# Block 8 of the attention stage: sigmoid issued ahead of block 0's layer norm, val chains in the four accumulator banks, conv in two halves

## The chip, the cores and the metric

One NeuronCore of a Trainium2 chip. Its engines are TensorE (PE in the profile, with its weight loads as PEld), VectorE (DVE), ScalarE (ACT), GpSimd (POOL) and SyncE (SP, which only issues DMAs here). The metric is the device time of one execution in microseconds; lower is better.

## The reference, cut to what matters

Three parts run one after the other over 4608 rows (8 x 576) of 512 channels: chunked attention, a gated convolution layer, and a layer norm with a feed-forward layer. The change lies at the seam of the second and third.

```python
x = attention(q, k, v)                              # chunks of 64, 8 heads of 64
gate = sigmoid(sum(conv_w[k] * x shifted by 4-k))   # 5 taps along the rows, per channel
y = (gate * (x @ w_val)) @ w_out
xn = (y - mean) / sqrt(var + 1e-6) * g_ln
out = y + relu(xn @ w_ch1) @ w_ch2
```

## The kernel before, in words

The rows are cut into 9 blocks of 512 (`BLK`, index j, 0 to 8), and each block into two units of 256 (`UN`, index u, 0 to 17). A loop over slots issues the first two parts: slot u computes unit u's scores (`a3`), transposes unit u-1's probabilities (`a4`) and multiplies them with v (`a5`, L208), which leaves the attention output of the block in `xf`, `xh` and `xl` with channels on partitions: four tiles of 128 channels, index f. The dense work of a block is spread over later slots by `at(slot, part, work)` (L655 to L672): `conv` (L243), `sigm` (L255), `val` (L266) and `proj` (L286).

- `conv(j, f, half)`: one ACT instruction (L248) and four DVE instructions (L250) over 512 columns, in place in `cg`. `half` 2 is all columns, 0 and 1 are the halves. Block 0 uses halves; all others are whole. There is one buffer of `cg`, shared by all blocks.
- `sigm(j)`: one ACT instruction over all of `cg` (L257).
- `val(j, f)`: a chain of 12 matmuls (three products per input tile, since each operand is split in a high and a low part) into one PSUM bank. Then DVE multiplies it with the gate (`gv`, L279), ACT copies the high part (`gh`, L282) and DVE subtracts to get the low part (`gl`, L283).
- `proj(j, t)`: a chain of 12 matmuls into one PSUM bank for 128 rows; ACT copies it to `y` (L296, two buffers) and issues the store to `y_dram` (L297).

All these chains take their bank from `ps_d`, a pool of two banks that are used in turn. PSUM has eight; the other six belong to `a3`, `a4` and `a5` until `prep()` (L620), called at the end of slot 18, closes their pools and opens `ps_t` (two banks, for transposes) and `acc` (four banks `acc0` to `acc3`, for the second feed-forward matmul, `ff2` at L372).

`prep()` also starts the third part for block 0: it loads block 0's `y` into `yt0` (L633), normalises four tiles of 128 rows (`ln_rows`, L317: statistics on DVE, a square root on ACT at L328, small DVE operations, then ACT at L337), transposes them on PE (`turn_rows`, L345), copies them out on ACT (L347), splits them into high and low (`high_low`, L389 and L390) and loads `yt0` again (L637). The first feed-forward matmul `ff1` (L354, tile `psh`) of block 0 reads the result.

What sets the order: from slot 4 on to the end of the slots, a planner orders each engine's queue. It runs through a model of the machine and takes, of what is ready, the work with the smallest place in program order; `tc.high_priority()` moves a piece's place forward. Each queue then runs strictly in that order on the chip. In the feed-forward part PE's order is the program's.

After the slots, `s_d.close()` (L684) gives back the memory of the weights `vh`, `vl`, `oh`, `ol` and of block buffers. The pools of the feed-forward part lie in the same memory and wait for its last readers tile by tile. There the weights of the feed-forward part are decoded, 16 tile pairs in all: loaded (L122, L127), decoded by ACT (L87) and three DVE passes (L88 to L90), split by ACT (L95) and POOL (L96). Those of the first four pairs are ready early; most of the rest run from 360 to 433 us.

Of the kernel before, what the change touches and what calls it, by code (L numbers as in the profile page):

```python
# [8 lines left out]
F32 = mybir.dt.float32  # L9
# [10 lines left out]
def tile_chunk_attention_gated_mlp(ctx: ExitStack, tc: tile.TileContext, qk, v, w_val, conv_w, w_out, g_ln, w1, w2, out):  # L20
# [10 lines left out]
    P = 128  # L31
    BLK = 512
    UN = 256
    UPB = BLK // UN
    NB = NT // BLK
# [12 lines left out]
    def boundary(j):  # L48
        o = (-(j * BLK)) % S
        return o if 0 < o < BLK else BLK  # L50
# [5 lines left out]
    ps_d = ctx.enter_context(tc.tile_pool(name="ps_d", bufs=2, space=PSUM))  # L56
# [186 lines left out]
    def conv(j, f, half):  # L243
        n = BLK + (HALO if boundary(j) < BLK else 0)
        x = xf[j]
        lo, hi = ((0, BLK // 2), (BLK // 2, n), (0, n))[half]
        o = cg[:, f, lo:hi]
        nc.scalar.activation(out=o, in_=x[:, f, lo:hi], func=ACTF.Copy, scale=cw[:, f:f + 1])  # L248
        for i in range(1, KC):
            nc.vector.scalar_tensor_tensor(  # L250
                out=o, in0=x[:, f, i + lo:i + hi], scalar=cw[:, i * CT + f:i * CT + f + 1], in1=o,
                op0=ALU.mult, op1=ALU.add,
            )

    def sigm(j):  # L255
        n = BLK + (HALO if boundary(j) < BLK else 0)
        nc.scalar.activation(out=cg[:, :, :n], in_=cg[:, :, :n], func=ACTF.Sigmoid)  # L257
# [3 lines left out]
    def chain(ps, ops):  # L261
        n = len(ops)
        for i, (lt, rh) in enumerate(ops):
            nc.tensor.matmul(out=ps, lhsT=lt, rhs=rh, start=(i == 0), stop=(i == n - 1))  # L264

    def val(j, f):  # L266
        hs, ls = wv["vs"]
        fs = slice(f * P, (f + 1) * P)
        ps = ps_d.tile([P, BLK], F32, tag="d", name="psv")
        ops = []  # L270
        for c in range(CT):
            ops += [(hs[c][:, fs], xh[j][:, c, :]), (hs[c][:, fs], xl[j][:, c, :]), (ls[c][:, fs], xh[j][:, c, :])]
        chain(ps, ops)
        o = boundary(j)
        gv = pD2.tile([P, BLK], F32, tag="gv", name="gv")
        with tc.high_priority():
            for lo, hi, sh in ((0, o, 0), (o, BLK, HALO)):
                if lo < hi:
                    nc.vector.tensor_tensor(out=gv[:, lo:hi], in0=ps[:, lo:hi], in1=cg[:, f, lo + sh:hi + sh], op=ALU.mult)  # L279
            a = pD1.tile([P, BLK], F32R, tag=f"gh{f}", name="gh")  # L280
            b = pD1.tile([P, BLK], F32R, tag=f"gl{f}", name="gl")
            nc.scalar.activation(out=a, in_=gv, func=ACTF.Copy)  # L282
            nc.vector.tensor_tensor(out=b, in0=gv, in1=a, op=ALU.subtract)  # L283
        gh[j, f], gl[j, f] = a, b

    def proj(j, t):  # L286
        hs, ls = wv["os"]
        ts = slice(t * P, (t + 1) * P)
        ps = ps_d.tile([P, DM], F32, tag="d", name="pso")
        ops = []  # L290
        for f in range(CT):
            ops += [(gh[j, f][:, ts], hs[f]), (gh[j, f][:, ts], ls[f]), (gl[j, f][:, ts], hs[f])]
        chain(ps, ops)
        y = pD2.tile([P, DM], F32, tag="y", name="y")
        with tc.high_priority():
            nc.scalar.activation(out=y, in_=ps, func=ACTF.Copy)  # L296
            nc.scalar.dma_start(out=y_dram[j][ts, :], in_=y)  # L297
# [4 lines left out]
    p2 = {}  # L302
# [14 lines left out]
    def ln_rows(ys):  # L317

        n = len(ys)
        mv = p2["b"].tile([P, n, 2], F32, tag="mv", name="mv")  # L320
        for t, y in enumerate(ys):
            s6 = p2["b"].tile([P, nc.vector.BN_STATS_DIM], F32, tag="s6", name="s6")
            nc.vector.bn_stats(out=s6, in_=y)
            nc.vector.bn_aggr(out=mv[:, t, :], in_=s6)
        ve = p2["b"].tile([P, n], F32, tag="ve", name="ve")
        nc.vector.tensor_scalar(out=ve, in0=mv[:, :, 1], scalar1=1e-6, scalar2=None, op0=ALU.add)
        r = p2["b"].tile([P, n], F32, tag="r", name="r")
        nc.scalar.activation(out=r, in_=ve, func=ACTF.Sqrt)  # L328
        nc.vector.reciprocal(out=r, in_=r)
        w = p2["b"].tile([P, n], F32, tag="w", name="w")  # L330
        nc.vector.tensor_tensor(out=w, in0=r, in1=r, op=ALU.mult)
        nc.vector.tensor_tensor(out=w, in0=w, in1=ve, op=ALU.mult)
        nc.vector.tensor_scalar(out=w, in0=w, scalar1=-0.5, scalar2=1.5, op0=ALU.mult, op1=ALU.add)
        nc.vector.tensor_tensor(out=r, in0=r, in1=w, op=ALU.mult)
        nc.vector.scalar_tensor_tensor(out=w, in0=mv[:, :, 0], scalar=-1.0, in1=r, op0=ALU.mult, op1=ALU.mult)
        for t, y in enumerate(ys):
            nc.scalar.activation(out=y, in_=y, func=ACTF.Identity, scale=r[:, t:t + 1], bias=w[:, t:t + 1])  # L337
        return ys

    def turn_rows(ys, i):  # L340

        for t, y in enumerate(ys):
            ps = ps_t.tile([P, CT, P], F32, tag="t", name="pst")
            for c in range(CT):
                nc.tensor.transpose(out=ps[:, c, :], in_=y[:, c * P:(c + 1) * P], identity=ident)  # L345
            for c in range(CT):
                nc.scalar.activation(  # L347
                    out=p2["xt"][:, c, (i + t) * P:(i + t + 1) * P], in_=ps[:, c, :], func=ACTF.Copy,
                    scale=cw[:, KC * CT + c:KC * CT + c + 1],
                )  # L350
# [19 lines left out]
    acc = {}  # L370
# [17 lines left out]
    def high_low(hi, lo, a, eng):  # L388
        nc.scalar.activation(out=hi, in_=a, func=ACTF.Copy)  # L389
        eng.tensor_tensor(out=lo, in0=a, in1=hi, op=ALU.subtract)  # L390
# [223 lines left out]
    def at(u, i, fn):  # L614
        dense.setdefault((u, i), []).append(fn)
# [4 lines left out]
    def prep():  # L620
        nonlocal xn0, yt0, ps_t
        s_a.close()
        ps_t = ctx.enter_context(tc.tile_pool(name="ps_t", bufs=2, space=PSUM, reuse_waits="tile"))
        p2["b"] = ctx.enter_context(tc.tile_pool(name="p2c", bufs=2, side="right", reuse_waits="tile"))
        pX = ctx.enter_context(tc.tile_pool(name="p2x", bufs=1, side="right", reuse_waits="tile"))
        p2["xt"] = pX.tile([P, CT, 2 * BLK], F32, name="xt")
        p2["0"] = s_0.enter_context(tc.tile_pool(name="p2a", bufs=1, side="right", reuse_waits="tile"))
        p2["h"] = s_0.enter_context(tc.tile_pool(name="p2h", bufs=2, side="right", reuse_waits="tile"))
        p2["acc"] = ctx.enter_context(tc.tile_pool(name="acc", bufs=1, space=PSUM, reuse_waits="tile"))
        xn0 = [p2["0"].tile([P, CT, BLK], F32R, name=f"xn{i}") for i in range(2)]  # L630
        yt0 = p2["0"].tile([P, HB, DM], F32, name="yt0")
        y0 = y_dram[0].rearrange("(t p) d -> p t d", p=P)
        nc.sync.dma_start(out=yt0, in_=y0)  # L633
        with tc.high_priority():
            ln_rows([yt0[:, i, :] for i in range(HB)])
        turn_rows([yt0[:, i, :] for i in range(HB)], 0)
        nc.sync.dma_start(out=yt0, in_=y0)  # L637
        for i in range(0, HB, 2):
            ts = slice(i * P, (i + 2) * P)
            high_low(xn0[0][:, :, ts], xn0[1][:, :, ts], p2["xt"][:, :, ts], nc.vector)  # L640
# [17 lines left out]
    for j in range(NB):  # L658
        u = UPB * (j + 1) + LAG - 1
        for f in range(CT):  # L660
            if j == NB - 1:
                at(u, 3, lambda j=j, f=f: conv(j, f, 2))
            elif j:
                at(*[(u, 3), (u, 3), (u + 1, 1), (u + 1, 1)][f], lambda j=j, f=f: conv(j, f, 2))
            else:
                at(u - 1, 3, lambda j=j, f=f: conv(j, f, 0))
                at(*[(u, 3), (u, 3), (u + 1, 0), (u + 1, 0)][f], lambda j=j, f=f: conv(j, f, 1))
        at(u + 1, 2, lambda j=j: sigm(j))
        for f in range(CT):
            at(*[(u + 1, 2), (u + 1, 3), (u + 2, 0), (u + 2, 1)][f], lambda j=j, f=f: val(j, f))  # L670
        for t in range(BLK // P):
            at(*[(u + 2, 2), (u + 2, 3), (u + 3, 0), (u + 3, 1)][t], lambda j=j, t=t: proj(j, t))  # L672
# [5 lines left out]
    for u in range(NU + LAG + 4):  # L678
        if u == MANUAL:
            head.close()  # L680
        slot(u)
        if u == NU + LAG - 1:
            prep()
    s_d.close()  # L684
    p2["w"] = ctx.enter_context(tc.tile_pool(name="wB", bufs=1, reuse_waits="tile"))
# [108 lines left out]
```

## Time and profile before

| | us |
|---|---|
| median of three runs | 1152.28 |
| lowest and highest of the three | 1148.00, 1153.68 |
| the profiled execution | 1149.92 |
| its span, first to last instruction | 1148.1 |
| PE busy in the span | 1076.7 (94%) |
| DVE busy | 710.6 (62%) |
| ACT busy | 483.1 (42%) |

The profiled execution's own time is 1.8 us more than its span. Busy time of an engine adds up instructions; a matmul of 512 columns is shown with 0.39 us though the next starts 0.23 us later at full clock, so PE's rate is read from the starts. PEclk is the clock granted to PE as a share of 2.4 GHz.

### The profile page before, as it was taken

How to read it: one execution, taken by the hardware profiler on the slowest of the kernel's cores; microseconds unless marked ns; L12 is line 12 of the kernel's file. 1: busy time of each engine (PE TensorE's matmuls, PEld its weight loads, DVE VectorE, ACT ScalarE, POOL GpSimd, SP SyncE). 2: the span in 40 equal slices, each digit the busy share in tenths (PEclk: the TensorE clock that was granted, in tenths of full speed). 3: DMA queues.
4: the chain of work that ended last, by engine and by line, in shares of the span. 5: the costliest groups of instructions: out<-in, count | busy, mean ns of one | idle time of the engine just before them, and what ended most of it. 6: DMA issues, size and time to landing. Idle time of an engine off the chain costs nothing.

```text
span 1148.1 us, 17073 instructions
## 1 busy us (share of the span) xinstructions
PE 1076.7 (94%) x6862; PEld 876.1 (76%) x6862; DVE 710.6 (62%) x1155; ACT 483.1 (42%) x828; POOL 110.8 (10%) x120
## 2 busy tenths in 40 slices
PE   5788989899869899899999999999999999999998
PEld 5676768777758787688887888887888888878877
DVE  6999899888664978555556544356444347432434
ACT  3566666556563665434534224333223324121221
POOL 2021010000002443322320000000000000000000
PEclk9799999999879999999999999999999999999999
DMA  8445546531123672723442723332623222722211
GB/s 330 167 127 168 176 140 211 172 132 56 41 89 133 209 235 80 250 110 127 148 148 92 238 91 124 97 110 92 227 85 129 101 74 97 233 92 83 83 37 74
DMA packets 58581, 155.28 MB, mean 135 GB/s; under 512 B 5742, under 2 KB 13958, under 8 KB 56198
## 3 DMA queue, kind: packets, MB, share of 16 engines
q1 hardware_dynamic: 53318, 144.75, 37.3%
q10 hardware_dynamic: 5184, 9.44, 2.2%
q8 instruction: 54, 0.88, 0.3%
q14 instruction: 25, 0.20, 0.1%
HBM read 116.41 MB, written 37.75 MB: 134 GB/s over the span
## 4 chain that ended last, share of the span: by engine, by line
PE 64%; DVE 23%; ACT 5%; issue 4%; DMA 3%; POOL 0%; SPq 0%; ACTq 0%; POOLq 0%; DVEq 0%
PE acc L496 15%; PE x L522 15%; PE psf L496 14%; PE zy L522 10%; DVE cg L250 7%; PE psv L264 5%; DVE da L90 2%; DVE da L89 2%; DVE sm L176 1%; PE acc L382 1%; DVE xl L238 1%; DVE h L534 1%; PE psh L264 1%; DVE pr L179 1%; DVE gv L279 1%
## 5 line engine op out<-in xcount | busy, mean ns | idle before, releaser
L542 DVE TENSOR_TENSOR c<-x,c 128x512 f32<-128x512 f32 x96 | 66.2, 690 | 236.9 <-ACT c L538 180.6
L496 PE MATMUL acc<-w,h 128*128 128x512 f32 x768 | 186.1, 391 | 0.0
L496 PE MATMUL psf<-w,h 128*128 128x512 f32 x768 | 186.0, 391 | 0.0
L496 PEld LDWEIGHTS acc<-w,h 128*128 128x128 f32 x768 | 144.2, 188 | 31.4
L496 PEld LDWEIGHTS psf<-w,h 128*128 128x128 f32 x768 | 144.2, 188 | 31.3
L522 PE MATMUL x<-t,wc 128*128 128x512 f32 x576 | 148.1, 393 | 3.4 <-DVE c L542 3.4
L538 ACT ACTIVATE c<-zy 128x512 f32<-128x512 f32 x96 | 57.9, 603 | 187.4 <-PE zy L522 187.2
L522 PEld LDWEIGHTS x<-t,wc 128*128 128x128 f32 x576 | 108.8, 189 | 27.8 <-DVE c L542 4.6
L533 ACT ACTIVATE h<-c 128x512 fp32r<-128x512 f32 x96 | 60.5, 631 | 136.3 <-DVE c L542 135.8
L250 DVE SCALAR_TENSOR_TENSOR cg<-xf,cw,cg 128x516 f32<-128x516 f32 (+2 forms) x160 | 106.3, 706 | 0.0
L501 DVE TENSOR_TENSOR yt<-psf,yt 128x512 f32<-128x512 f32 x128 | 88.2, 691 | 25.1 <-PE psf L496 21.1
L522 PE MATMUL zy<-b,wc 128*128 128x512 f32 x384 | 98.9, 393 | 0.0
L264 PE MATMUL psv<-xh,vh 128*128 128x512 f32 x144 | 64.2, 446 | 22.6 <-DVE gv L279 22.6
L522 PEld LDWEIGHTS zy<-b,wc 128*128 128x128 f32 x384 | 71.2, 188 | 14.6
L534 DVE SCALAR_TENSOR_TENSOR h<-c,h 128x512 fp32r<-128x512 f32 x96 | 68.4, 713 | 14.1 <-ACT h L533 13.9
L96 POOL TENSOR_TENSOR w<-da,w 128x512 fp32r<-128x512 f32 x32 | 49.2, 1543 | 142.3 <-ACT w L95 137.7
L264 PE MATMUL psv<-xl,vh 128*128 128x512 f32 x144 | 61.4, 426 | 0.0
L264 PE MATMUL psv<-xh,vl 128*128 128x512 f32 x144 | 61.1, 424 | 0.0
L264 PE MATMUL pso<-oh,gh 128*128 128x512 f32 x144 | 58.3, 405 | 0.1
L264 PE MATMUL pso<-oh,gl 128*128 128x512 f32 x144 | 56.3, 392 | 0.3 <-DVE gl L283 0.3
L264 PE MATMUL pso<-ol,gh 128*128 128x512 f32 x144 | 56.1, 391 | 0.0
L390 POOL TENSOR_TENSOR wc<-raws,wc 128x256 fp32r<-128x256 f32 x56 | 45.1, 827 | 107.4 <-ACT wc L389 100.7
(108 smaller groups left out, 1566.5 us busy)
## 6 DMA issues: line engine op xcount, KB each, us to landing
wc<-wc SPq DMA_DIRECT2D x112, 512.0 KB, 3.3
qkr<-in_qk SPq DMA_DIRECT2D x18, 1024.0 KB, 6.0
raw<-in_moe_w_ch SPq DMA_DIRECT2D x32, 512.0 KB, 4.2
vr<-in_v SPq DMA_DIRECT2D x18, 512.0 KB, 4.3
yd<-y ACTq DMA_DIRECT2D x36, 256.0 KB, 3.0
out<-yt SPq DMA_DIRECT2D x36, 256.0 KB, 3.8
yr<-yd SPq DMA_DIRECT2D x32, 256.0 KB, 3.0
yt<-yd SPq DMA_DIRECT2D x32, 256.0 KB, 4.3
```

What stands on the lines that cost most here:

```text
L89: nc.vector.scalar_tensor_tensor(out=au, in0=hw, scalar=0x80000000, in1=au, op0=ALU.bitwise_and, op1=ALU.bitwise_or)
L96: nc.gpsimd.tensor_tensor(out=lo, in0=a, in1=hi, op=ALU.subtract)
L250: nc.vector.scalar_tensor_tensor(out=o, in0=x[:, f, i + lo:i + hi], scalar=cw[:, i * CT + f:i * CT + f + 1], in1=o, op0=ALU.mult, op1=ALU.add,
L264: nc.tensor.matmul(out=ps, lhsT=lt, rhs=rh, start=(i == 0), stop=(i == n - 1))
L390: eng.tensor_tensor(out=lo, in0=a, in1=hi, op=ALU.subtract)
L496: nc.tensor.matmul(out=ps, lhsT=lt, rhs=rh, start=(g == 0 and k == 0 and (first or half)), stop=(g == 1 and k == 2 and (last or half)),)
L501: nc.vector.tensor_tensor(out=yt[i], in0=ps, in1=yt[i], op=ALU.add)
L522: nc.tensor.matmul(out=ps, lhsT=lt, rhs=rh, start=(start and c == 0 and i == 0), stop=(c == 1 and i == 2), skip_group_check=True)
L533: nc.scalar.activation(out=t[:, 0, :], in_=src, func=ACTF.Relu)
L534: nc.vector.scalar_tensor_tensor(out=t[:, 1, :], in0=src, scalar=0.0, in1=t[:, 0, :], op0=ALU.max, op1=ALU.subtract)
L538: nc.scalar.activation(out=t, in_=zy, func=ACTF.Copy)
L542: nc.vector.tensor_tensor(out=t, in0=x, in1=t, op=ALU.add)
```

## The change

For the last block (j = 8) only: `val` takes its four banks from the pool `acc` in place of `ps_d`; `conv` is issued in two halves, the first before the second unit's attention output is there; `sigm` is issued at high priority ahead of `prep()` and no longer in slot 19.

```diff
--- before.py
+++ after.py
@@ -266,7 +266,10 @@
     def val(j, f):
         hs, ls = wv["vs"]
         fs = slice(f * P, (f + 1) * P)
-        ps = ps_d.tile([P, BLK], F32, tag="d", name="psv")
+        if j == NB - 1:
+            ps = p2["acc"].tile([P, BLK], F32, tag=f"acc{f}", name="psv")
+        else:
+            ps = ps_d.tile([P, BLK], F32, tag="d", name="psv")
         ops = []
         for c in range(CT):
             ops += [(hs[c][:, fs], xh[j][:, c, :]), (hs[c][:, fs], xl[j][:, c, :]), (ls[c][:, fs], xh[j][:, c, :])]
@@ -659,13 +662,15 @@
         u = UPB * (j + 1) + LAG - 1
         for f in range(CT):
             if j == NB - 1:
-                at(u, 3, lambda j=j, f=f: conv(j, f, 2))
+                at(u, 1, lambda j=j, f=f: conv(j, f, 0))
+                at(u, 3, lambda j=j, f=f: conv(j, f, 1))
             elif j:
                 at(*[(u, 3), (u, 3), (u + 1, 1), (u + 1, 1)][f], lambda j=j, f=f: conv(j, f, 2))
             else:
                 at(u - 1, 3, lambda j=j, f=f: conv(j, f, 0))
                 at(*[(u, 3), (u, 3), (u + 1, 0), (u + 1, 0)][f], lambda j=j, f=f: conv(j, f, 1))
-        at(u + 1, 2, lambda j=j: sigm(j))
+        if j < NB - 1:
+            at(u + 1, 2, lambda j=j: sigm(j))
         for f in range(CT):
             at(*[(u + 1, 2), (u + 1, 3), (u + 2, 0), (u + 2, 1)][f], lambda j=j, f=f: val(j, f))
         for t in range(BLK // P):
@@ -680,6 +685,8 @@
             head.close()
         slot(u)
         if u == NU + LAG - 1:
+            with tc.high_priority():
+                sigm(NB - 1)
             prep()
     s_d.close()
     p2["w"] = ctx.enter_context(tc.tile_pool(name="wB", bufs=1, reuse_waits="tile"))
```

## Rows read from the trace of the kernel before

**Rows 1.** The page, parts 1 and 4: engine totals; chain by engine
```profile
PE 1076.7 (94%) x6862; PEld 876.1 (76%) x6862; DVE 710.6 (62%) x1155; ACT 483.1 (42%) x828; POOL 110.8 (10%) x120
...
PE 64%; DVE 23%; ACT 5%; issue 4%; DMA 3%; POOL 0%; SPq 0%; ACTq 0%; POOLq 0%; DVEq 0%
```

**Rows 2.** Busy time by stretch, between val(8,1) and proj(8)
```profile
core 0: us, PE busy (x) PEld busy (x) DVE busy (x) ACT busy (x) POOL busy (x), PEclk, DMA share, GB/s
...
328.62:341.57 12.95, 3.62 (x17) 2.27 (x16) 4.28 (x6) 11.99 (x25) 0.00 (x0) 0.64 0.24 82
341.57:345.95 4.38, 4.37 (x11) 3.47 (x11) 1.84 (x3) 1.22 (x2) 0.00 (x0) 0.51 0.00 0
```

**Rows 3.** Timeline, PE: start, length, work, [idle before <- releaser]
```profile
328.39 0.39 PE L264 MATMUL psv<-xh,vl 128*128 128x512 f32 x1
329.23 1.36 PE L345 MATMUL pst<-ident,yt 128*128 128x128 f32 x8 [0.45 <-ACT yt L337]
332.36 2.15 PE L345 MATMUL pst<-ident,yt 128*128 128x128 f32 x8 [1.77 <-ACT xt L347]
341.58 0.79 PE L264 MATMUL psv<-xh,vh 128*128 128x512 f32 x1 [7.07 <-DVE gv L279]
...
345.95 0.40 PE L264 MATMUL psv<-xl,vh 128*128 128x512 f32 x1
```

**Rows 4.** The chain of waits, 300 to 362 us: start, length, what
```profile
328.36 2.93 ACT yt L337 x4
...
337.59 1.28 ACT L257
...
338.89 1.92 ACT cg L257
...
340.83 0.70 DVE gv L279
```

**Rows 5.** Timeline of PE: proj(8) and the first of psh
```profile
349.13 0.39 PE L264 MATMUL pso<-oh,gh 128*128 128x512 f32 x1
...
360.04 1.33 PE L264 MATMUL psh<-xn,w 128*128 128x512 f32 x5
```

**Rows 6.** Timeline of PE at full clock: eight transposes in a row
```profile
409.09 1.04 PE L345 MATMUL pst<-ident,yr 128*128 128x128 f32 x8
```

**Rows 7.** Timeline of DVE, 300 to 330 us: conv(8)
```profile
322.52 2.07 DVE L250 SCALAR_TENSOR_TENSOR cg<-xf,cw,cg 128x512 f32<-128x512 f32 x3
...
328.29 1.54 DVE L250 SCALAR_TENSOR_TENSOR cg<-xf,cw,cg 128x512 f32<-128x512 f32 x2
```

**Rows 8.** Timeline of DVE, 34 to 52 us: block 0's conv in half columns
```profile
51.10 1.27 DVE L250 SCALAR_TENSOR_TENSOR cg<-xf,cw,cg 128x256 f32<-128x256 f32 x3
```

**Rows 9.** Busy time of all engines while block 7's val chains run
```profile
300.00:316.00 16.00, 13.54 (x105) 10.81 (x106) 6.91 (x14) 7.98 (x11) 0.00 (x0) 0.79 0.17 46
```

**Rows 10.** Timeline of ACT, 326 to 361 us
```profile
331.20 2.14 ACT L347 ACTIVATE xt<-pst,cw 128x128 f32<-128x128 f32 x8
...
359.06 0.60 ACT L296 ACTIVATE y<-pso 128x512 f32<-128x512 f32 x1 [3.66 <-DMA yd<-y]
...
360.74 0.62 ACT L95 ACTIVATE w<-da 128x512 fp32r<-128x512 f32 x1
```

**Rows 11.** Timeline of SP's queue, 300 to 362 us
```profile
334.59 0.38 SPq L637 DMA_DIRECT2D yt<-yd  x1
349.32 0.81 SPq L703 DMA_DIRECT2D yr<-yd  x2
```

**Rows 12.** Busy time: PE over four acc banks; the decode stretch
```profile
437.64:443.35 5.71, 5.71 (x25) 4.69 (x25) 3.92 (x5) 4.93 (x8) 2.74 (x3) 0.97 0.23 92
360.05:433.26 73.21, 66.93 (x297) 53.97 (x296) 61.58 (x120) 47.18 (x100) 33.86 (x22) 0.98 0.62 197
```

**Rows 13.** Line 90, a decode's last DVE pass: ns min/median/max, starts
```profile
L90 DVE SCALAR_TENSOR_TENSOR da<-raw,da x40: 640/683/1784, 11.0 to 435.8; 128x512 uint32<-128x512 uint32 x40
```

## The prediction

> **What bounds the kernel now.** The page comes first: PE is busy 94% of the span, and the chain that ended last is PE for 64% and DVE for 23% [rows 1]. So only a stretch where PE stands still, or runs at the low clock, can give time back. The second view is busy time by stretch at the seam that the change touches. In the 12.95 us from 328.62 PE is busy 3.62 us, and in the next 4.38 us it is busy but at a granted clock of 0.51, the lower level of 1.2 GHz [rows 2]. PE's timeline shows what happens: val(8,1) issues its last matmul at 328.39, block 0's 16 transposes follow in two bursts, and val(8,2) starts only at 341.58, released by `gv`; its first ten matmuls then take until 345.95 [rows 3]. The chain of waits says why `gv` is late: ACT normalises block 0 from 328.36, copies its transposes out and splits them, loads the sigmoid's table at 337.59 and runs the sigmoid at 338.89; `gv` follows at 340.83 [rows 4]. The conv that feeds the sigmoid had ended at 328.29 + 1.54 = 329.83 [rows 7]. So nine of those microseconds are a place in ACT's queue, and val(8,2) waits for `gv` only because `ps_d` has two banks.
>
> **Part 1, the four banks.** val(8,2) and val(8,3) no longer need a bank that `gv` must empty; the `acc` banks are not used by `ff2` until much later. PE's work from 328.62 on is then two val chains, 16 transposes and four proj chains. A matmul of a chain starts every (360.04 - 349.13) / 48 = 0.227 us [rows 5], eight transposes take 1.04 us [rows 6]. Sum: 24 x 0.227 + 2 x 1.04 + 10.91 = 18.4 us, so psh starts at 347.1, not at 360.04: **13.0 us**. The same from what goes away: 12.95 - 2.08 = 10.9 us of standing still [rows 2], and ten matmuls in 4.37 us in place of 2.27 [rows 3], 2.1 us.
>
> **Part 2, the conv.** 16 DVE instructions of 512 columns at 2.07 / 3 = 0.69 us [rows 7] become 32 of 256 columns at 1.27 / 3 = 0.42 us [rows 8]: 13.5 us for 11.0. The second half alone is 6.8, so the conv ends 4.3 us earlier, at 325.5, if the first half is hidden. Its cover is DVE's idle time beside block 7's val chains, 16.00 - 6.91 = 9.1 us [rows 9], against 6.8 needed. `cg` is one buffer, so tile f waits for block 7's `gv` of f, and f = 3 has only the last of those gaps. Without the cover the conv ends at 332.3. The first half's four ACT instructions lie there too, where ACT is busy 7.98 of 16.00 us [rows 9]. The Trainium skill (VectorE: DVE Perf Modes, the section on the TRN2 errata) speaks against this part: small operands pay a fixed latency each, and it advises tiles of 512 or more; by its formula a pair of halves costs 0.06 us more than a whole, 1.0 us in all, where the rows give 2.5. Both are covered, so the sum is the same by either.
>
> **Part 3, the sigmoid.** At 325.5 it needs no table load if it goes ahead of the square root, since the table of block 7's is still there; it ends 1.9 us later, at 327.4, or 334.2 without the cover of part 2. PE needs its result for proj(8,0), after `gv` (0.70 us [rows 4]) and two steps of about the same size, at 336.1 by part 1. So the sigmoid costs nothing with the cover, and at most 0.2 us without.
>
> **What is late next.** Behind the sigmoid on ACT now stand the square root and its table load, block 0's normalisation, transposes' copies and split. The sigmoid (1.92) and the load (1.28) push them back by up to 3.2 us [rows 4]. Now the last transpose ends at 332.36 + 2.15 = 334.51 [rows 3], which is 334.51 - 328.62 - 2.08 = 3.8 us later than without waits. If the planner leaves them between val(8,1) and val(8,2), PE waits up to 3.8 + 3.2 = 7.0 us; if it lets val(8,2) and val(8,3) run in the meantime, nothing. I take **1.0**, near the lower end, because those two chains now wait for nothing and the planner takes what is ready. The copies, 2.14 us for eight [rows 10], and the split end well ahead of 347.
>
> Two queues are passed. SP reloads `yt0` at 334.59 (L637) and loads the next rows at 349.32 (L703), 14.7 us apart [rows 11]; after the change both come within a few us, with the raw weights behind them. The copy of y(8,2) already waited 3.66 us for the store of y(8,0) at 359.06 [rows 10], and psh needs its bank. That can cost another 0 to 3.7 us; I take **0.5**, as the reload should be through before the first store. On POOL nothing moves but the start of the decode: ACT's L95 at 360.74 stands right behind the last y copies [rows 10], since its destination lies in memory that proj(8) reads. It moves forward with proj(8), and with it the whole stretch to 433, in which PE is busy 66.93 of 73.21 us and DVE 61.58 [rows 12]. A second square root table load later on falls away too; ACT is not the bound there, so I count nothing.
>
> **Sum:** 13.0 - 1.0 - 0.5 = 11.5 us. The profiled execution, 1149.92 us, would become 1138.4. It lies 2.4 us under the median of the three runs; the four known times average 1151.0, and I take that as the base: **1139.5 us**.
>
> **Rivals.**
> *The sigmoid stays where it is on ACT* (the change does not do what it says): the planner's model has the conv late and lets the normalisation go first. The val chains still run on, but PE stands from 336.1. The gate comes at 340.83 as now; four `gv` and four `gl` at 0.7 us on DVE put the last `gl` at 346.4, and 36 more matmuls, 8.2 us, end proj(8) at 354.6: 5.4 us saved, 1145.6. For it: all of those pieces are at high priority. Against: its place in program order is ahead, and its input is ready first.
> *Given back at PE's transposes and at the stores:* half of both upper bounds, 3.5 and 1.85, leaves 7.7 us: 1143.3. For it: the two bursts of transposes waited for ACT twice [rows 3], and stores are late already.
> *PE drops to the low clock over four banks:* val(8,0) to val(8,3) at 0.437 us a matmul [rows 3] cost 48 x 0.21 = 10.1 us more, which leaves 1.4 saved: 1149.6. The Trainium skill (TensorE: Matmul & The Clock Gate, "A second HAM failure mode: psum-queue depth-cycling") reports a kernel whose clock oscillates as it cycles through PSUM banks. The trace speaks against it: `ff2`'s 24 matmuls over the same four banks take 5.71 us at a granted clock of 0.97 [rows 12].
> *Slower:* the decode stretch. A decode's last pass on DVE has a median of 0.683 us, but single ones take up to 1.784, 1.1 us more [rows 13]; I take it that these are the ones beside POOL's subtractions (POOL is busy 33.86 us of 73.21 [rows 12]). Moved forward, more passes may fall beside them. DVE has 73.21 - 61.58 = 11.6 us of slack there, and 11.5 are gained before it, so it decides from 21 more stretched passes of the 60 on; with 30 the kernel is 9.9 us slower, 1160.9. Against it: the order of work in that stretch stays as it is.
> *Nothing:* a gap that opens again elsewhere, 1151.
>
> **How the numbers follow.** Chances: the forecast 0.60; sigmoid in place 0.12; given back 0.15; low clock 0.02; nothing 0.05; slower 0.06. About 0.5% (5.8 us) is what a measurement of this kernel can tell from no change. Faster by more: the forecast, most of the given-back case and a part of the first rival, 0.78. Slower by more: 0.06. The rest, 0.16. The range: the whole 13.0 us, on an execution as fast as the fastest run (1148.0), gives 1135.0; the other end takes in the given-back case and the sigmoid in place with their scatter, 1147.0.
>
> **What would show it.** Right: val(8,2) starts 0.23 us after val(8,1), PE stands for less than 2 us between 323 and 347, the granted clock stays at 1.00 there, psh starts near 348, no table load stands ahead of block 8's sigmoid, and the decode stretch behind psh is as long as before, 73 us. Wrong: PE waits for `gl` of block 8 (first rival), for `yt` or `xt` between val chains, or for y's copy at psh (second); the granted clock falls in the val chains (third); the stretch after psh grows (fourth).

## The result and the profile after

The changed kernel takes **1136.52 us** (median of 4 runs, 1135.95 to 1138.29) against 1152.94 of the kernel before (4 runs beside them): ratio 0.987, interval 0.9854 to 0.9886. Its profiled execution is 1135.95 us, with a span of 1134.2; before it was 1149.92 and 1148.1. The forecast, 1139.5 and faster, was right, and so was its sum of PE's work at the seam. Which edit earns the gain it had wrong: the part costed at nothing brings most of it when it is applied alone.

The page of the changed kernel, busy time of each engine and the chain that ended last, answers to [rows 1]:

```profile
PE 1070.5 (94%) x6862; PEld 871.4 (77%) x6862; DVE 712.8 (63%) x1171; ACT 483.5 (43%) x832; POOL 110.6 (10%) x120
...
PE 65%; DVE 24%; issue 4%; ACT 3%; DMA 3%; POOL 0%; SPq 0%; ACTq 0%; POOLq 0%; DVEq 0%
```

The shares hardly move; DVE has 2.2 us more than before. To see where time went, cut the span at events that both kernels have. One is the pair of bursts in which PE multiplies the probabilities of block 8's second unit with v (`x<-pT,vr`, 18 and 46 matmuls, with 24 matmuls of val(7) between them); the next is the first matmul of `psh`; then the first of `zy`. Call the stretch from the second burst to `psh` **the seam**: it holds proj(7), val(8), block 0's transposes and proj(8). Busy time by stretch, the changed kernel, then the kernel before; rows are first burst to second burst, and the seam:

```profile
core 0: us, PE busy (x) PEld busy (x) DVE busy (x) ACT busy (x) POOL busy (x), PEclk, DMA share, GB/s
302.38:308.52 6.14, 6.14 (x42) 4.84 (x43) 6.10 (x16) 2.84 (x6) 0.00 (x0) 1.00 0.01 3
308.52:344.01 35.49, 35.49 (x207) 29.51 (x207) 23.19 (x54) 24.36 (x45) 0.00 (x0) 1.00 0.41 145
```

```profile
302.46:311.31 8.85, 8.85 (x43) 6.84 (x43) 3.23 (x8) 1.78 (x3) 0.00 (x0) 0.67 0.01 2
311.31:360.04 48.73, 39.39 (x207) 31.57 (x207) 24.26 (x45) 25.20 (x44) 0.00 (x0) 0.86 0.32 108
```

In the seam the same 207 matmuls take 48.73 - 35.49 = **13.2 us** less; PE is busy all of it and the granted clock is 1.00. Ahead of the seam 2.7 us went as well, and behind it 2.0 came back (`psh` to `zy` takes 101.9 us, before 99.9). With 0.1 gained ahead of the first burst and 0.1 lost behind `zy` that is the 13.9 us between the spans. Neither of the two outer differences is shown to belong to the change: both vary as much between executions of the changed kernel (the repeats below and the last section). The kernel before was traced once, so its own seam has no repeat.

PE's timeline of the changed kernel answers to [rows 3] (start, length, work):

```profile
327.42 0.39 PE L264 MATMUL psv<-xl,vh 128*128 128x512 f32 x1
327.65 0.60 PE L348 MATMUL pst<-ident,yt 128*128 128x128 f32 x4
328.00 0.48 PE L264 MATMUL psv<-xh,vl 128*128 128x512 f32 x1
328.32 0.60 PE L348 MATMUL pst<-ident,yt 128*128 128x128 f32 x4
...
332.19 0.60 PE L348 MATMUL pst<-ident,yt 128*128 128x128 f32 x4
...
333.34 0.60 PE L348 MATMUL pst<-ident,yt 128*128 128x128 f32 x4
...
344.01 1.32 PE L264 MATMUL psh<-xn,w 128*128 128x512 f32 x5
```

The two bursts of eight transposes, which waited and then left PE standing, have become four of four, strewn among the matmuls of val(8) and proj(8), and none waits. ACT's and DVE's timelines of the changed kernel answer to [rows 4, 7] (lines behind L268 lie three lower than before: L340 is L337 of before):

```profile
318.85 1.28 ACT L331 ACT_TABLE_LOAD   x1 [0.39 <-ACT y L299]
320.15 0.21 ACT L331 ACTIVATE r<-ve 128x4 f32<-128x4 f32 x1
...
321.57 1.28 ACT L257 ACT_TABLE_LOAD   x1 [0.39 <-ACT y L299]
323.87 1.92 ACT L257 ACTIVATE cg<-cg 128x2048 f32<-128x2048 f32 x1 [1.01 <-DVE cg L250]
325.69 1.50 ACT L340 ACTIVATE yt<-yt,w,r 128x512 f32<-128x512 f32 x2
...
343.17 0.60 ACT L299 ACTIVATE y<-pso 128x512 f32<-128x512 f32 x1 [3.80 <-DMA yd<-y]
...
345.12 0.60 ACT L299 ACTIVATE y<-pso 128x512 f32<-128x512 f32 x1 [1.35 <-DMA yd<-y]
345.61 0.62 ACT L95 ACTIVATE w<-da 128x512 fp32r<-128x512 f32 x1
```

```profile
323.35 0.48 DVE L250 SCALAR_TENSOR_TENSOR cg<-xf,cw,cg 128x256 f32<-128x256 f32 x1
323.75 0.16 DVE L338 SCALAR_TENSOR_TENSOR w<-mv,r 128x4 f32<-128x4 f32 x1
325.82 1.29 DVE L282 TENSOR_TENSOR gv<-psv,cg 128x512 f32<-128x512 f32 x2 [1.92 <-ACT cg L257]
```

The sigmoid now stands ahead of the normalisation, and DVE's rows show which of the two inputs was ready first: the conv's last half ends at 323.83, the normalisation's last scale (L338) at 323.91. In the kernel before, the last scale (there L335) was ready at 328.33, ACT's normalisation began at 328.36 [rows 4], and the conv ended only at 329.83 [rows 7]; DVE's row of that scale:

```profile
328.18 0.15 DVE L335 SCALAR_TENSOR_TENSOR w<-mv,r 128x4 f32<-128x4 f32 x1
```

The square root still went first, so the sigmoid's table load did not go away; it moved to 321.57, where ACT had nothing else to do. ACT's last lines after the change show one thing that got worse: the copies of y(8,2) and y(8,3) wait 3.80 + 1.35 us for the stores, and L95 behind them starts 1.6 us after `psh`, before 0.7 [rows 5, 10].

### The profile page after: what moved, and what is told of

It reads as the page before. It is cut to its first block, busy times and chain, and to the rows that moved or that the text cites. A ratio compares the mean times of both kernels' runs of the same rounds, so it can differ in the third digit from the quotient of the medians.

```text
span 1134.2 us, 17091 instructions
## 1 busy us (share of the span) xinstructions
PE 1070.5 (94%) x6862; PEld 871.4 (77%) x6862; DVE 712.8 (63%) x1171; ACT 483.5 (43%) x832; POOL 110.6 (10%) x120
## 4 chain that ended last, share of the span: by engine, by line
PE 65%; DVE 24%; issue 4%; ACT 3%; DMA 3%; POOL 0%; SPq 0%; ACTq 0%; POOLq 0%; DVEq 0%
PE acc L499 16%; PE x L525 15%; PE psf L499 14%; PE zy L525 10%; DVE cg L250 7%; PE psv L264 5%; DVE da L89 2%; DVE da L90 2%; DVE sm L176 2%; PE acc L385 1%; DVE xl L238 1%; DMA raw<-in_moe_w_ch 1%; DVE h L537 1%; PE psh L264 1%; DVE mx L167 1%
## 5 line engine op out<-in xcount | busy, mean ns | idle before, releaser
L250 DVE SCALAR_TENSOR_TENSOR cg<-xf,cw,cg 128x516 f32<-128x516 f32 (+1 forms) x176 | 108.6, 661 | 0.0
L525 PE MATMUL zy<-b,wc 128*128 128x512 f32 x384 | 98.9, 393 | 0.0
L537 DVE SCALAR_TENSOR_TENSOR h<-c,h 128x512 fp32r<-128x512 f32 x96 | 68.5, 713 | 14.0 <-ACT h L536 13.9
```

The lines of the kernel that those rows point to most:

```text
L250: nc.vector.scalar_tensor_tensor(out=o, in0=x[:, f, i + lo:i + hi], scalar=cw[:, i * CT + f:i * CT + f + 1], in1=o, op0=ALU.mult, op1=ALU.add,
L525: nc.tensor.matmul(out=ps, lhsT=lt, rhs=rh, start=(start and c == 0 and i == 0), stop=(c == 1 and i == 2), skip_group_check=True)
L537: nc.vector.scalar_tensor_tensor(out=t[:, 1, :], in0=src, scalar=0.0, in1=t[:, 0, :], op0=ALU.max, op1=ALU.subtract)
```

## The experiments

Each run is set beside the kernel before. `psh` to `zy` and the seam are in us, from the timelines of the profiled execution.

| run | what it has | median (runs) | ratio, 95% | seam | psh to zy |
|---|---|---|---|---|---|
| before | | 1150.15 to 1152.94 | 1 | 48.73 | 99.9 |
| after | all three parts | 1136.52 (4) | 0.987, 0.9854 to 0.9886 | 35.49 | 101.9 |
| e1_banks | banks alone | 1145.66 (9) | 0.9948, 0.9932 to 0.9965 | 43.58 | 99.3 |
| e2_sigm | sigmoid's call alone | 1145.91 (6) | 0.9958, 0.9941 to 0.9974 | 42.96 | 100.3 |
| e3_halves | conv halves alone | 1138.85 (4) | 0.9899, 0.9879 to 0.9919 | 36.45 | 98.4 |
| e4_no_halves | banks, call | 1139.2 (4) | 0.9901, 0.9881 to 0.9921 | 37.04 | 98.9 |
| e5_no_sigm | banks, halves | 1137.97 (4) | 0.9889, 0.9867 to 0.9912 | 35.66 | 98.9 |
| e6_no_banks | call, halves | 1140.35 (4) | 0.9908, 0.9885 to 0.9932 | 36.45 | 99.3 |
| r_after_again | after | 1139.5 (4) | 0.9901, 0.9872 to 0.9929 | 35.64 | 101.1 |
| e7_y4 | after, y in gv's buffers | 1135.67 (4) | 0.9873, 0.9838 to 0.9909 | 35.49 | 98.4 |
| e8_reload | after, reload later | 1136.65 (4) | 0.9875, 0.9849 to 0.9901 | 35.50 | 99.2 |
| e9_both | e7 and e8 | 1139.84 (6) | 0.9903, 0.988 to 0.9926 | 35.49 | 100.8 |
| r_after_third | after | 1139.65 (6) | 0.9897, 0.9875 to 0.992 | 35.49 | 99.5 |
| e10_lean | halves, y in gv's buffers | 1136.39 (5) | 0.987, 0.9848 to 0.9892 | 36.38 | 99.0 |

The seam repeats to 0.15 us over three executions of the changed kernel, while the median of its whole time moves by 3 us from one comparison to the next. So the parts are read from the seam.

### Each part alone

**Banks.**

```diff
-        ps = ps_d.tile([P, BLK], F32, tag="d", name="psv")
+        if j == NB - 1:
+            ps = p2["acc"].tile([P, BLK], F32, tag=f"acc{f}", name="psv")
+        else:
+            ps = ps_d.tile([P, BLK], F32, tag="d", name="psv")
```

> Only the four banks; conv whole, sigmoid at its old place. Theory (the gain is PE's wait, and the place of the sigmoid in ACT's queue sets it): val(8,2) and val(8,3) run on, but proj(8,0) waits for gl of block 8, since the gate still comes near 341; psh starts near 354.6 and about 5.4 us are saved, ratio 0.995. Rival (the banks are the cause and the rest only helps): most of the gain is here, psh before 348, ratio 0.989 or less.

PE's waits in this kernel around the seam (releaser, then us in total, times, longest), and its ACT and DVE timelines:

```profile
PE pso L264 <- ACT gh L285: 5.4, 1, 5.4
```

```profile
329.54 2.93 ACT L340 ACTIVATE yt<-yt,w,r 128x512 f32<-128x512 f32 x4 [4.39 <-DVE w L338]
...
338.50 1.28 ACT L257 ACT_TABLE_LOAD   x1
339.80 1.91 ACT L257 ACTIVATE cg<-cg 128x2048 f32<-128x2048 f32 x1
```

```profile
329.35 0.15 DVE L338 SCALAR_TENSOR_TENSOR w<-mv,r 128x4 f32<-128x4 f32 x1
329.47 1.54 DVE L250 SCALAR_TENSOR_TENSOR cg<-xf,cw,cg 128x512 f32<-128x512 f32 x2
```

The four val chains run on, but the sigmoid keeps its place behind the normalisation, whose scales are ready 1.5 us before the conv, and PE then stands 5.39 us ahead of proj(8,0). Saved in the seam: 48.73 - 43.58 = 5.15 us. This is the prediction's first rival almost to the number (5.4), and the run's own theory.

**The sigmoid's call.**

```diff
-        at(u + 1, 2, lambda j=j: sigm(j))
+        if j < NB - 1:
+            at(u + 1, 2, lambda j=j: sigm(j))
...
         if u == NU + LAG - 1:
+            with tc.high_priority():
+                sigm(NB - 1)
             prep()
```

> Only the sigmoid ahead; val in ps_d, conv whole. Theory: the conv ends near 329.8, the gate near 332, so val(8,2) waits for its bank until about 332.6 in place of 341.6; with the transposes in the gap some 2 us of standing still are left; 9 to 11 us saved, ratio 0.991. Rival (banks are the cause): two banks keep PE waiting, less than 5 us saved, ratio 0.996 or more.

ACT's timeline of this kernel, then PE's:

```profile
327.79 2.23 ACT L337 ACTIVATE yt<-yt,w,r 128x512 f32<-128x512 f32 x3 [4.39 <-DVE w L335]
330.03 1.28 ACT L257 ACT_TABLE_LOAD   x1
331.32 1.91 ACT L257 ACTIVATE cg<-cg 128x2048 f32<-128x2048 f32 x1
```

```profile
334.01 0.80 PE L264 MATMUL psv<-xh,vh 128*128 128x512 f32 x1 [3.99 <-DVE gv L279]
334.60 0.63 PE L264 MATMUL psv<-xl,vh 128*128 128x512 f32 x1
335.03 0.63 PE L264 MATMUL psv<-xh,vl 128*128 128x512 f32 x1
335.46 0.63 PE L264 MATMUL psv<-xh,vh 128*128 128x512 f32 x1
```

High priority lifts the sigmoid past one normalisation of four and past the transposes' copies, but not past what is ready before its conv has ended. PE still stands 3.99 us for `gv`, and the matmuls that follow start 0.43 us apart, not 0.227, with transposes of block 0 after four of them: the slow restart that was seen before [rows 3] stays in part. Saved: 5.77 us, where the run's theory had 9 to 11 and its rival less than 5.

**The conv's halves.**

```diff
             if j == NB - 1:
-                at(u, 3, lambda j=j, f=f: conv(j, f, 2))
+                at(u, 1, lambda j=j, f=f: conv(j, f, 0))
+                at(u, 3, lambda j=j, f=f: conv(j, f, 1))
```

> Only the conv in halves. Theory: the sigmoid stands behind block 0's normalisation on ACT, so an earlier conv moves nothing after it: 0 us, ratio 1.000 within 0.003. Rival (the conv is on the path): 4 us saved, ratio 0.996. On block 7's val chains: if their full clock in the changed kernel comes from the halves, all 24 matmuls from val(7,2) on start 0.227 us apart here too; if it is chance, it comes and goes among these runs without regard to the halves.

DVE's timeline of this kernel, then ACT's, then PE's one wait in the seam:

```profile
326.68 0.48 DVE L250 SCALAR_TENSOR_TENSOR cg<-xf,cw,cg 128x256 f32<-128x256 f32 x1
327.08 0.15 DVE L335 SCALAR_TENSOR_TENSOR w<-mv,r 128x4 f32<-128x4 f32 x1
```

```profile
327.19 1.92 ACT L257 ACTIVATE cg<-cg 128x2048 f32<-128x2048 f32 x1 [1.00 <-DVE cg L250]
329.02 1.50 ACT L337 ACTIVATE yt<-yt,w,r 128x512 f32<-128x512 f32 x2
```

```profile
329.87 0.66 PE L345 MATMUL pst<-ident,yt 128*128 128x128 f32 x4 [0.54 <-ACT yt L337]
```

Saved: 48.73 - 36.45 = **12.3 us** of the 13.2, by the part to which the prediction gave nothing of its own. The conv now ends (327.16) before the scales (327.23), so the planner puts the sigmoid first of itself, with no change to its call; then `gv` empties the two banks of `ps_d` in time and val(8,2) does not wait. Counted from the second burst, the sigmoid ends at 17.3 us (329.11 - 311.85) in place of 29.5 (340.80 - 311.31), 12.2 us earlier. The earlier end of the conv is 3.2 us of that; the other 9.0 are the sigmoid's place on ACT. In all eight kernels with the halves, with the call or without, the sigmoid stands ahead of all four normalisations, in all four without them behind three or four. That the planner does this because of what is ready first in its model is inferred from this order; no run shows the planner's own steps. The theory that the banks earn the gain and the conv only has to stay hidden falls here.

### Each part left out

These are the changed kernel with one part undone: the minus lines of the diffs above restored in place of the plus lines, for the halves (e4), the sigmoid's call (e5) and the banks (e6).

> Banks and sigmoid, conv whole again (the change without its halves). Theory: the gate comes near 332 in place of 325.8 but PE needs it only for proj(8,0) near 334 to 336, so at most 1 us is lost against the changed kernel: ratio to before 0.987 to 0.989. Rival (conv on the path): 4 us lost, ratio 0.9905.

> Banks and halves, the sigmoid at its old place in program order and without priority. New theory (the planner takes what is ready: an earlier end of the conv alone puts the sigmoid ahead of block 0's normalisation): the same as the changed kernel, ratio to before 0.987 to 0.990, sigmoid on ACT ahead of the four normalisations. Old theory (the sigmoid's call and priority do it): the gate near 341, ratio 0.995.

> Sigmoid and halves, val in ps_d. New theory: gv(8,0) comes before val(8,2) needs its bank, so the banks are not needed: ratio 0.987 to 0.990, PE waits for no gv of block 8. Rival (the banks carry a part of their own): 2 us or more slower than the changed kernel, PE waits for gv of block 8.

Without the halves, ACT's timeline has the same order as in e2, and four banks cover it:

```profile
327.56 2.23 ACT L340 ACTIVATE yt<-yt,w,r 128x512 f32<-128x512 f32 x3 [4.38 <-DVE w L338]
329.81 1.28 ACT L257 ACT_TABLE_LOAD   x1
331.11 1.92 ACT L257 ACTIVATE cg<-cg 128x2048 f32<-128x2048 f32 x1
```

e4 saves 11.7 us in the seam; PE waits 0.23 us for `yt` and 0.80 for a copy of y ahead of `psh`. It saves 1.4 to 1.6 us less than all three parts together, a little more than the 1 us expected to be lost. Without the call nothing is lost: e5's seam is 35.66 against 35.49 to 35.64 of the three executions with all parts, and e6's is e3's, 36.45 both. Without the banks 0.8 to 1.0 us is lost (36.45 against 35.49 or 35.66), of which 0.54 is the wait for `yt` that e3's row shows; in e3 against the first profile the other 0.42 lies in PE's busy time (35.91 us against 35.49, both at a granted clock of 1.00) and was not traced to an instruction. So there are two ways to the gain, the halves, or the banks with the call, and with the halves in place the call is worth nothing that shows and the banks about 0.9 us.

### The stores of y, and repeats

The changed kernel was run twice more, to see what of the first comparison lies outside the change.

> The changed kernel once more, unchanged, for a second trace. If the full clock of block 7's val chains in its first trace was chance, some of the 24 matmuls before x(17) start 0.43 us apart here and the stretch from x's first to its second burst is near 8.9 us as in the four other kernels, and the time stands 2 to 3 us above the first profiled one. If it belongs to the change, the stretch is 6.1 us again.

> The changed kernel again, on the same chip as the two above. PE's part from x's second burst to psh is 35.5 us as in its other traces; the parts before and after it vary by about 2 to 3 us with the granted clock.

Busy time by stretch, first repeat, from the first burst to the second (columns as above); the row answers to the one of 6.14 us at a granted clock of 1.00 in the first profile:

```profile
301.47:310.49 9.02, 9.02 (x43) 7.00 (x43) 6.30 (x16) 2.84 (x6) 0.00 (x0) 0.65 0.01 2
```

So the 2.7 us ahead of the seam do not come with the change as such: the third execution has 8.95. Of the six traces with all three parts two are short there, the first and e7's (6.17), and four take 8.8 to 9.0, as do all eight others. Behind the seam, `psh` to `zy` took 101.9, 101.1 and 99.5 us.

Then the copies that wait for stores: first two more buffers for y, then `yt0`'s second load, which I held to be what the stores collide with, moved to step 9 of the feed-forward loop, then both.

```diff
-        y = pD2.tile([P, DM], F32, tag="y", name="y")
+        y = pD2.tile([P, DM], F32, tag="gv" if j == NB - 1 and t > 1 else "y", name="y")
```

```diff
-        nc.sync.dma_start(out=yt0, in_=y0)
...
         next_ff(f + NFA + 1)
+        if f == 9:
+            nc.sync.dma_start(out=yt0, in_=y_dram[0].rearrange("(t p) d -> p t d", p=P))
```

> The changed kernel with y of block 8's third and fourth tile in the two buffers of gv, so that their copies wait for no store. Theory (the decode stretch gave back about 2 us because its first ACT instruction, L95, stands behind copies that wait for stores): L95 comes within 1 us of psh's start in place of 1.6, PE waits in the decode stretch shrink, about 1 us faster than the changed kernel, ratio 0.9865. Rival (the raw weights' loads set it): no difference, ratio as the changed kernel.

> The changed kernel with the second load of yt0 moved from the end of prep to the middle of the decode stretch. Theory (that load, now issued within half a microsecond of the next loads, is what makes the stores of y late): the copies of y(8,2) and y(8,3) wait about as long as in the kernel before (3.7 us in all in place of 5.2), L95 comes 0.7 us after psh's start in place of 1.5. Rival (the stores are late without it): L95 still 1.2 us or more after psh. The total moves by 1 us at most under either.

> The changed kernel with both: y in gv's buffers and the later load of yt0. Theory: no copy of block 8 waits for a store, PE's part from psh to zy as in the run with y in gv's buffers alone (98.4 us), so the load's place adds nothing to it; 0 to 2 us faster than the changed kernel. Rival: each gives a part, 2 us or more.

ACT's timeline of e7, then of e8:

```profile
344.62 0.60 ACT L299 ACTIVATE y<-pso 128x512 f32<-128x512 f32 x1 [2.12 <-PE pso L264]
345.11 0.62 ACT L95 ACTIVATE w<-da 128x512 fp32r<-128x512 f32 x1
```

```profile
345.22 0.60 ACT L299 ACTIVATE y<-pso 128x512 f32<-128x512 f32 x1 [3.83 <-DMA yd<-y]
347.34 0.60 ACT L299 ACTIVATE y<-pso 128x512 f32<-128x512 f32 x1 [1.52 <-DMA yd<-y]
347.83 0.62 ACT L95 ACTIVATE w<-da 128x512 fp32r<-128x512 f32 x1
```

e7 removes the waits: the copies wait for PE alone, and L95 starts 0.7 us after `psh`. e8 removes nothing (3.83 + 1.52 us, L95 1.8 us after), so the reload is not what makes the stores late; that reason of mine falls, and whether another load does it was not tried. On the total, e7, e8 and e9 cannot be told from the changed kernel: their intervals overlap, and `psh` to `zy` is 98.4 and 100.8 with the extra buffers, 99.2 with the reload alone. In e7 and in e9 no copy waits for a store, and still the stretch differs by 2.4 us, against e9's theory. Whether the late L95 costs anything stays open.

The last run joins the part that earns most with the buffers, and leaves banks and call out.

> The kernel before with the conv in halves and y in gv's buffers, without the banks and without the sigmoid's new place. Theory (the halves do the work): within 2 us of the kernel with y in gv's buffers and all three edits, ratio to before 0.986 to 0.991; from x's second burst to psh 36.5 us as with the halves alone. Rival (the banks keep a part): 3 us or more behind it.

It gives 0.987, the same as the changed kernel's best, from two edits: halves and buffers. No run's ratio is clearly below the changed kernel's. On the same chip, though, e10's five executions (1135.16 to 1136.71 us) all lie below the six of e9 (1138.11 to 1141.04), which has all three parts, the buffers and the later reload. So the banks and the call show no gain on top of the halves in the total, and why e9 is slower stays open.

## Why the prediction was right, and where not

- **13.0 us in the seam**: 13.2 measured. The sum held: PE's work, one matmul every 0.227 us, with no waits and no low clock.
- **"val(8,2) waits for `gv` only because `ps_d` has two banks"**: the step that failed. With two banks and the halves val(8,2) does not wait (e3, 12.3 us saved); with four banks alone 5.15 us are saved, and on top of the halves the banks bring about 0.9. The prediction did say that the rest hangs on the sigmoid's early place, but it looked for that in part 3's call. The banks with the call are a second way, not the only one (e4, 11.7 us). The call alone does not put the sigmoid ahead: with the conv whole its input is not ready first (e2).
- **Part 2 costed at nothing, its cover DVE's idle time**: the cost was right (seam at PE's bound, DVE busy 6.10 of 6.14 us ahead of it in place of 3.23 of 8.85), the gain was missed. It had worked out that the conv ends 4.3 us earlier; counted from the second burst, the end came at 323.83 - 308.52 = 15.3 us against 329.83 - 311.31 = 18.5, 3.2 earlier. What it did not ask is which of two ready times on DVE this changes the order of. The two rows stand side by side in the kernel before: the scale at 328.18, then the last conv instructions at 328.29 [rows 7].
- **DVE's cost of the halves**: 2.5 us by rows, 2.2 measured (712.8 against 710.6 [rows 1]). By the formula of the Trainium skill (VectorE: DVE Perf Modes, the section on the TRN2 errata) the estimate was 1.0; the section itself notes that this formula gives too little for a single operation, and the measurement decides for the rows.
- **Part 3, no table load if the sigmoid goes ahead of the square root**: the square root went first, and the load at 321.57 is hidden by ACT's idle time. The later table load that was to fall away stayed: 19 loads before and after. The sigmoid still ended at 325.79, 17.3 us after the second burst, well before proj(8,0).
- **1.0 us for the transposes**: 0. They were placed between the matmuls of val(8) and proj(8).
- **0.5 us for the stores**: nothing in the seam; the waits grew from 3.66 to 5.15 us, but PE did not wait for them. The sum, 11.5, was 1.7 us under the 13.2.
- **Low clock over four banks**: did not come. The 207 matmuls of the seam ran at 1.00, so this rival's 10.1 us stayed away. The oscillation that the Trainium skill reports (TensorE: Matmul & The Clock Gate, "A second HAM failure mode: psum-queue depth-cycling") comes with short idle times of PE between groups of matmuls. In the seam PE has none (busy 35.49 of 35.49 us), so the seam does not test it.
- **Slower by the decode stretch**: `psh` to `zy` took 98.4 to 101.9 us in all runs, 99.9 before; the 9.9 us of that rival did not come.
- **The total**: three medians of the changed kernel, 1136.52, 1139.5 and 1139.65, lie within 3.0 us of the forecast, 1139.5, and inside the range. That one of them equals it to the digit is luck: the seam gave 1.7 us more than the sum, and the stretches around it vary by 2 to 3 us. Against the kernel before beside each, the medians differ by 16.4, 11.9 and 10.5 us, where the sum had 11.5.

## What to carry to other kernels

Where a planner takes what is ready, the order on one engine can hang on which input is ready first on another: find the two producers' last rows, and see which edit swaps them. Raising the priority did not bring the sigmoid ahead while its input was not there, and finishing the input 3 us earlier did what the priority could not. Run each part of a change alone: here the three bring 5.2, 5.8 and 12.3 us and together 13.2, because each attacks the same wait.

## What of the hardware was not expected

The clock that is granted after the same wait differs between executions of the same program. In every profile PE waits 3.07 or 3.08 us for `pT` ahead of the first burst. After it the next 42 matmuls (the burst and the 24 of val(7)) ran at a granted clock of 1.00 and took 6.14 us in the first profile of the changed kernel, and at 0.65 and 9.02 us in the second. That is 2.9 us between two executions of one program. The kernel before has 8.85 us there, so 2.7 of the 13.9 us between the first two spans, a fifth, is no more than such executions differ by.
